# Windowed attention and a mixture-of-depths layer on one core: value matmul in two 64-column tiles, sinks in two 32-row tiles, double PSUM banks, loads in another order

## The chip, the core and the metric

The kernel runs on one core of a Trainium2 chip. A core has five engines, each with its own in-order instruction stream: TensorE (PE, matrix products into PSUM, the accumulator memory of eight banks), VectorE (DVE), ScalarE (ACT), GpSimd (POOL) and SyncE (SP, which here only issues transfers). PEld is TensorE's load of the stationary operand (the weights of a matmul), shown apart from the matmul (PE) that streams the moving operand past it. Sixteen DMA engines move data between the device's memory and SBUF, the on-chip memory; transfers are issued on POOL's queue, which may change the type on the way, or on SP's. The metric is the device time of one execution in microseconds (us), lower is better.

## The reference

Attention in which each query sees 128 keys up to its own and the first four keys (the sinks), followed by a layer that lets only the 128 tokens with the highest score of each batch through a small network.

```
B, H, S, D = 4, 8, 768, 64;  n_sink, window = 4, 128
scores = (q @ k^T) / sqrt(D)
keep = (pos_k < n_sink) | ((0 <= pos_q - pos_k) & (pos_q - pos_k < window))
a = exp(where(keep, scores, -1e9) - max);  a = a / (sum(a) + 1e-9)
x = concat_heads(a @ v)                      # (4, 768, 512)
# layer: w1 is 512 x 1024, w2 is 1024 x 512, capacity 128
s = x @ w_gate;  top = the 128 tokens of a batch with the largest s
out = x;  out[top] = x[top] + sigmoid(s[top]) * (relu(x[top] @ w1) @ w2)
```

## The kernel before

**Staging.** q and k of a batch come through POOL's queue, cast from f32 to bf16 (`load_qk`, L77: four pieces of 192 KB each for batch 0, one of 768 KB each for the others); v and the sinks' v come as f32 through SP's (`load_v`, L87 and L89). `transposes` (L147) turns 128 x 64 blocks of q and k on TensorE, two heads into the two halves of a tile of PSUM (64 output partitions, hence 64 weight columns, each), and DVE and ACT copy the result to KT and QT; the first four keys go to `ksk`.

**Attention.** The work runs over 24 units (b, j): batch b, block j of 128 queries. `scores` (L170, L177, L180) computes for a block kc of keys the transposed scores of its own and the next query block, for four heads at a time (group g): keys are the output's partitions, so the exponentials `pt` are the weights of the value matmul without another transpose. ACT takes the exponential from one bank (512 columns) at a time; POOL zeroes what the window excludes (L184, L188). `sink_scores` does the sinks of a whole batch at once. `pv` (L214) multiplies: weights `pt` (128 keys x 128 queries, f32), moving operand v of one head and a column of ones (65 columns, f32), output 128 queries x 65 columns, whose last column is the softmax's sum. A unit has 16 such matmuls (8 where j is 0), since the window spans two key blocks. The sinks' part of a unit is one matmul for each group (L206), 128 weight rows of which most are zero, 260 columns. `finish_block` divides by the sum (L223, L225), computes the score s (L228) and a bf16 copy (L231).

**Layer.** `moe_gen` is a generator: the layer of batch b is fed in steps, two in each unit, between the matmuls of batch b + 1; that of the last batch runs at the end alone. Its steps: broadcast s over partitions (dg on DVE L243, bc on TensorE L244, sbc on ACT L246); rank every token by counting greater scores, six times one DVE pass over 768 columns (L254) and a comparison that makes a one-hot block E (L257); transpose E (etp, L263); gather the chosen tokens (xeT, L271); w1 and Relu (hps, L290, L292); w2 (ye, L296); scatter back (ops, L303) and add x (o_sb, L305); store.

**Order.** In each unit the code writes the scores of the next unit ahead of `pv` of this one, then `finish_block`, then one pair of heads of the next batch's transposes (units 1 to 4). The build's scheduler places instructions on each engine, by data dependences and free buffers, and may move them from where the code writes them; from there on every engine runs its stream in order. Buffers: `sc_ps` two tiles of one bank (scores), `x_ps` two tiles of two banks (value), `mo_ps` two tiles of one bank (transposes and everything of the layer).

Of the kernel before, what the change touches and what calls it, by code (L numbers as in the profile page):

```python
# [15 lines left out]
H = 8  # L16
S = 768
# [11 lines left out]
def kernel(  # L29
# [27 lines left out]
    x_ps = ctx.enter_context(tc.tile_pool(name="x_ps", bufs=2, space=bass.MemoryType.PSUM))  # L57
    mo_ps = ctx.enter_context(tc.tile_pool(name="mo_ps", bufs=2, space=bass.MemoryType.PSUM))
# [3 lines left out]
    vsk = [vp.tile([128, H, VS], FP32, name=f"vsk{i}", tag=f"vsk{i}") for i in range(2)]  # L62
# [19 lines left out]
    def load_v(st):  # L82
        b = st.b
        st.v = vbuf[b % 2]
        st.vsk = vsk[b % 2]
        for h in range(H):
            nc.sync.dma_start(out=st.vsk[4 * h:4 * h + 4, h, 0:D], in_=v[b, h, 0:NSINK, :])  # L87
        for c in range(NB):
            nc.sync.dma_start(out=st.v[:, c, :, 0:D],  # L89
                              in_=v[b, :, c * 128:(c + 1) * 128, :].rearrange("h p d -> p h d"))  # L90

    st0 = load_qk(0, 4)

# [12 lines left out]
    for i in range(2):  # L106
        nc.gpsimd.affine_select(
            out=vsk[i][0:32, :, D:D + 1].rearrange("p h o -> p (h o)"),
            in_=ones_f[0:32, 0:H], compare_op=ALU.is_ge, fill=0.0, base=0,
            pattern=[[-4, H]], channel_multiplier=1)  # L110
        nc.gpsimd.affine_select(
            out=vsk[i][0:32, :, D:D + 1].rearrange("p h o -> p (h o)"),
            in_=vsk[i][0:32, :, D:D + 1].rearrange("p h o -> p (h o)"),
            compare_op=ALU.is_ge, fill=0.0, base=3,
            pattern=[[4, H]], channel_multiplier=-1)
    load_v(st0)
# [21 lines left out]
    def transposes(st, hp):  # L138
# [4 lines left out]
        for src, dst, eng in ((st.kb, st.KT, "v"), (st.qb, st.QT, "s")):  # L143
            trp = mo_ps.tile([128, NB, 128], BF16, name="trp", tag="mo")
            for c in range(NB):
                for e in range(2):
                    nc.tensor.transpose(out=trp[64 * e:64 * e + 64, c, :], in_=src[:, 2 * hp + e, c, :],  # L147
                                        identity=ident_b[:])
            o = dst[:, hp, :].rearrange("d (p c) -> d p c", c=NB)
            i = trp[:, :, :].rearrange("d c p -> d p c")  # L150
            if eng == "v":
# [3 lines left out]
        for e in range(2):  # L155
            nc.vector.tensor_copy(
                out=st.ksk[64 * e:64 * e + 64, hp, 8 * hp + 4 * e:8 * hp + 4 * e + 4],
# [3 lines left out]
    def scores(st, kc, g):  # L161
# [4 lines left out]
        banks = [sc_ps.tile([128, 2, 256], FP32, name="sc", tag="sc") for _ in range(2)]  # L166
        for hh in range(2):
            for e in range(2):
                hp = 2 * g + hh
                nc.tensor.matmul(  # L170
                    out=banks[e][:, hh, 0:nq],
# [3 lines left out]
        for e in range(2):  # L175
            if kc == 0:
                nc.tensor.matmul(out=banks[e][:, :, :], lhsT=ident_b[:, :], rhs=mask0[:, :, :],  # L177
                                 start=False, stop=True, skip_group_check=True)
            po = pt[:, 4 * g:4 * g + 4, :].rearrange("p (a e) n -> p e a n", e=2)
            nc.scalar.activation(out=po[:, e, :, 0:nq], in_=banks[e][:, :, 0:nq],  # L180
                                 func=ACT.Exp, scale=0.125)
# [10 lines left out]
    def sink_scores(st):  # L192
        st.psk = sp.tile([128, 512], FP32, name="psk", tag="psk")
        sk = mo_ps.tile([128, 512], FP32, name="sk", tag="mo")
        for hp in range(HP):
            nc.tensor.matmul(out=sk[:, :], lhsT=st.ksk[:, hp, :], rhs=st.QT[:, hp, 256:S],  # L196
                             start=(hp == 0), stop=(hp == HP - 1))
        nc.scalar.activation(out=st.psk[:, :], in_=sk[:, :], func=ACT.Exp, scale=0.125)

    def pv(st, j, g):  # L200
        if g == 0:
            st.xg = x_ps.tile([128, 2, 512], FP32, name="xg", tag="xg")
        xg = st.xg
        first = True
        if j >= 2:
            nc.tensor.matmul(out=xg[:, g, 0:4 * VS], lhsT=st.psk[:, (j - 2) * 128:(j - 1) * 128],  # L206
                             rhs=st.vsk[:, 4 * g:4 * g + 4, :].rearrange("p h e -> p (h e)"),
                             start=True, stop=False, skip_group_check=True)
            first = False
        for hh in range(4):  # L210
            h = 4 * g + hh
            terms = [(j, 0)] if j == 0 else [(j - 1, 128), (j, 0)]
            for kc, off in terms:
                nc.tensor.matmul(out=xg[:, g, hh * VS:(hh + 1) * VS],  # L214
                                 lhsT=st.pt[kc][:, h, off:off + 128],
                                 rhs=st.v[:, kc, h, :], start=first, stop=(hh == 3 and kc == j),
                                 skip_group_check=True)
                first = False

    def finish_block(st, j):  # L220
# [166 lines left out]
```

## Time and profile before

| | |
|---|---|
| median of 3 runs | 237.33 us (237.24 to 238.42) |
| profiled execution | 238.03 us, span 236.3 us |
| busy, share of the span | PE 83%, PEld 65%, DVE 50%, ACT 38%, POOL 25% |
| mean granted TensorE clock | 0.888 of full speed |
| chain that ended last | PE 74% (of the span: value matmul L214 36%, sinks 8%, scores 7%), waits for `kb` 12%, DVE 5% |
| transfers | 21.56 MB, 91 GB/s mean |

The span runs from the first to the last instruction. Busy time is the time in which an engine had an instruction under way, whatever else was waiting; matmuls are pipelined, and their ends are modelled, so a fully busy PE isn't an array at its peak. The chain is the sequence of work and waits that ended last, followed back from the end. The granted clock is 1.00 at 2.4 GHz and 0.50 at 1.2.

### The profile page before, as it was taken

What the parts mean: (1) busy time and instruction counts of PE and PEld (TensorE: products, weight loads), DVE (VectorE), ACT (ScalarE), POOL (GpSimd) and SP (SyncE); (2) the same over time, 40 slices, a digit from 0 to 9 for tenths busy, and PEclk for the clock granted to TensorE, in tenths of its full rate; (3) what the DMA queues carried; (4) which work ended last, traced back from release to release, by engine and by line L of the source; (5) the groups of instructions that cost most, each with busy time, mean ns of one, the idle gap of its engine ahead of it and who ended that gap; (6) DMA issues with size and microseconds to landing.
All of it is one profiled execution on the core that took longest, in us unless ns stands there. A gap on an engine that the chain in (4) does not pass through costs nothing.

```text
span 236.3 us, 4345 instructions
## 1 busy us (share of the span) xinstructions
PE 196.0 (83%) x1752; PEld 154.7 (65%) x1752; DVE 118.5 (50%) x292; ACT 90.4 (38%) x169; POOL 59.1 (25%) x101
## 2 busy tenths in 40 slices
PE   0369701999999999999999999999999999944850
PEld 0344401887887888887878788777888977922810
DVE  3542100330444199853746896287399607488032
ACT  2124700232354474454365545544465533120210
POOL 8901410032225046223103442210054223000000
PEclk9999955555699999999999999999999999985595
DMA  7999999995122991202434000033000004200024
GB/s 108 182 200 199 194 191 219 206 188 97 46 47 48 181 177 44 46 1 68 186 109 89 0 3 3 0 137 133 0 3 0 3 0 163 106 0 0 4 106 162
DMA packets 38821, 21.56 MB, mean 91 GB/s; under 512 B 25872, under 2 KB 35088, under 8 KB 38800
## 3 DMA queue, kind: packets, MB, share of 16 engines
q0 software_dynamic: 9984, 8.39, 23.1%
q1 hardware_dynamic: 28816, 12.88, 21.8%
q8 instruction: 14, 0.23, 0.4%
q14 instruction: 7, 0.06, 0.1%
HBM read 23.36 MB, written 6.29 MB: 125 GB/s over the span
## 4 chain that ended last, share of the span: by engine, by line
PE 74%; DMA 13%; DVE 5%; POOL 4%; issue 1%; ACT 1%; POOLq 0%; DVEq 0%
PE xg L214 36%; DMA kb<-in_k_dram 12%; PE xg L206 8%; PE sc L170 7%; PE trp L147 5%; PE hps L290 4%; PE ye L296 3%; PE bc L244 3%; PE xeT L271 3%; DVE cjunk L254 2%; PE ops L303 2%; PE sc L177 1%; POOL qb L77 1%; POOL kb L77 1%; PE sk L196 1%; DVE o_sb L305 1%
## 5 line engine op out<-in xcount | busy, mean ns | idle before, releaser
L214 PEld LDWEIGHTS xg<-vbuf,pt 128*128 128x128 f32 x704 | 92.9, 205 | 8.6 <-issue 5.4
L214 PE MATMUL xg<-vbuf,pt 128*128 128x65 f32 x704 | 96.7, 289 | 0.0
L180 ACT ACTIVATE pt<-sc 128x512 f32<-128x512 f32 (+1 forms) x96 | 50.3, 562 | 53.6 <-PE sc L170 47.2
L184 POOL TENSOR_SCALAR_AFFINE_SELECT pt<-pt 128x512 f32<-128x512 f32 x40 | 25.6, 641 | 131.8 <-ACT pt L180 131.8
L223 DVE RECIPROCAL rz<-xg 128x8 f32<-128x8 f32 x24 | 4.9, 205 | 65.4 <-PE xg L214 65.3
L147 PE MATMUL trp<-ident_b,kb 128*64 128x128 bf16 x192 | 10.4, 257 | 22.5 <-DMA kb<-in_k_dram 14.3
L154 ACT COPY QT<-trp 128x768 bf16<-128x768 bf16 x16 | 12.8, 802 | 32.8 <-PE trp L147 32.8
L254 DVE TENSOR_SCALAR_CACHE_REDUCE cjunk<-sbc,scol 128x768 f32<-128x768 f32 x24 | 24.1, 1004 | 1.8 <-ACT sbc L246 1.8
L170 PE MATMUL sc<-QT,KT 64*128 64x256 bf16 (+1 forms) x192 | 24.3, 281 | 0.7 <-ACT pt L180 0.7
L147 PEld LDWEIGHTS <-kb 128*64 128x64 bf16 x192 | 7.4, 130 | 25.2 <-DMA kb<-in_k_dram 22.4
L228 DVE CUSTOM_DVE_ANT_0 junk<-x,wgb 128x512 f32<-128x512 f32 x24 | 16.5, 687 | 14.7 <-DMA wgb<-in_moe_w_gate_dram 14.4
L206 PE MATMUL xg<-vsk,psk 128*128 128x260 f32 x64 | 22.5, 435 | 0.0
L305 DVE TENSOR_TENSOR o_sb<-ops,x 128x512 f32<-128x512 f32 x24 | 15.7, 688 | 10.9 <-PE ops L303 9.5
L188 POOL TENSOR_SCALAR_AFFINE_SELECT pt<-pt 128x512 f32<-128x512 f32 x32 | 20.3, 634 | 0.0
L152 DVE COPY KT<-trp 128x768 bf16<-128x768 bf16 x16 | 15.3, 954 | 8.8 <-PE trp L147 8.8
L231 ACT CAST xb<-x 128x512 bf16<-128x512 f32 x24 | 14.8, 619 | 9.8 <-DVE x L225 9.8
L225 DVE TENSOR_TENSOR x<-xg,rz 128x512 f32<-128x512 f32 x24 | 16.5, 686 | 0.4
L206 PEld LDWEIGHTS xg<-vsk,psk 128*128 128x128 f32 x64 | 10.7, 196 | 5.0 <-issue 2.5
L170 PEld LDWEIGHTS <-KT 64*128 64x128 bf16 x192 | 7.1, 95 | 10.4 <-issue 6.6
L147 PE MATMUL trp<-ident_b,qb 128*64 128x128 bf16 x192 | 10.8, 256 | 1.1 <-DVE KT L152 1.1
L263 PE MATMUL etp<-ident_b,E 128*128 128x128 bf16 x24 | 5.7, 237 | 6.2 <-DVE E L257 6.2
L303 PE MATMUL ops<-gye,ET 128*128 128x512 bf16 x24 | 8.3, 380 | 3.0 <-DVE o_sb L305 2.3
(57 smaller groups left out, 164.4 us busy)
## 6 DMA issues: line engine op xcount, KB each, us to landing
vbuf<-in_v_dram SPq DMA_DIRECT2D x24, 256.0 KB
out_dram<-o_sb SPq DMA_DIRECT2D x24, 256.0 KB
qb<-in_q_dram POOLq DMA_DIRECT2D x3, 768.0 KB, 24.4
kb<-in_k_dram POOLq DMA_DIRECT2D x3, 768.0 KB, 9.1
w_sb<-in_moe_w_dram POOLq DMA_DIRECT2D x2, 1024.0 KB, 16.9
qb<-in_q_dram POOLq DMA_DIRECT2D x4, 192.0 KB, 7.7
kb<-in_k_dram POOLq DMA_DIRECT2D x4, 192.0 KB, 8.4
vsk<-in_v_dram SPq DMA_DIRECT2D x32, 1.0 KB
```

Of the source, the lines that this page charges most:

```text
L147: nc.tensor.transpose(out=trp[64 * e:64 * e + 64, c, :], in_=src[:, 2 * hp + e, c, :], identity=ident_b[:])
L152: nc.vector.tensor_copy(out=o, in_=i)
L170: nc.tensor.matmul(out=banks[e][:, hh, 0:nq], lhsT=st.KT[64 * e:64 * e + 64, hp, kc * 128:(kc + 1) * 128], rhs=st.QT[64 * e:64 * e + 64, h ...
L180: nc.scalar.activation(out=po[:, e, :, 0:nq], in_=banks[e][:, :, 0:nq], func=ACT.Exp, scale=0.125)
L184: nc.gpsimd.affine_select(out=pt[:, hs, 0:128], in_=pt[:, hs, 0:128], compare_op=ALU.is_ge, fill=0.0, base=0, pattern=[[0, 4], [1, 128]], ...
L188: nc.gpsimd.affine_select(out=pt[:, hs, 128:256], in_=pt[:, hs, 128:256], compare_op=ALU.is_ge, fill=0.0, base=-1, pattern=[[0, 4], [-1, 1 ...
L206: nc.tensor.matmul(out=xg[:, g, 0:4 * VS], lhsT=st.psk[:, (j - 2) * 128:(j - 1) * 128], rhs=st.vsk[:, 4 * g:4 * g + 4, :].rearrange("p h e ...
L214: nc.tensor.matmul(out=xg[:, g, hh * VS:(hh + 1) * VS], lhsT=st.pt[kc][:, h, off:off + 128], rhs=st.v[:, kc, h, :], start=first, stop=(hh ...
L225: nc.vector.tensor_tensor(out=xn, in0=xv[:, :, :, 0:D], in1=rz[:, :, :, :].to_broadcast((128, 2, 4, D)), op=ALU.mult)
L228: nc.vector.tensor_tensor_reduce(out=junk[:, :], in0=st.x[:, j, :], in1=wgb[:, :], scale=1.0, scalar=0.0, op0=ALU.mult, op1=ALU.add, accum ...
L254: nc.vector.tensor_scalar(out=cjunk[:, :], in0=sbc[:, :], scalar1=scol[:, c:c + 1], scalar2=0.0, op0=ALU.is_gt, op1=ALU.add, accum_out=ran ...
L305: nc.vector.tensor_tensor(out=o_sb[:, :], in0=ops[:, :], in1=st.x[:, c, :], op=ALU.add)
```

## The change

- **Value matmul** (`pv`): each product is split by its queries into two matmuls of 64 weight columns, m = 0 into the PSUM partitions 0 to 63, m = 1 into 64 to 127, both with the same 65 moving columns. Groups have their own tile of one bank (`x_ps`, three of them); the reciprocal and the division are done for each group, right behind its matmuls.
- **Sinks**: the sinks' weights and values of the groups lie in rows 0 to 31 and 32 to 63, and `pv_sinks` issues both groups' matmuls in a row, ahead of `pv`, each on 32 rows.
- **Banks**: `sc_ps` holds two tiles of two banks, used by the scores of four heads (one Exp over 1024 columns instead of two over 512), the transposes (k and q in one tile), the sinks' scores, bc (one tile and one copy for six blocks), hps (one tile, one Relu over 1024 columns) and ops (two blocks and one addition over 1024 columns at a time). `mo_ps` is one bank, for etp, xeT, se and ye.
- **Order**: the scores of both groups of the next unit are written ahead of this unit's value matmuls; `sink_scores` of a batch comes behind its unit 0; w1 and w2 are loaded in the program's second unit; v of batch 0 is loaded through POOL's queue, right behind q and k.

```diff
-    x_ps = ctx.enter_context(tc.tile_pool(name="x_ps", bufs=2, space=bass.MemoryType.PSUM))
-    mo_ps = ctx.enter_context(tc.tile_pool(name="mo_ps", bufs=2, space=bass.MemoryType.PSUM))
+    x_ps = ctx.enter_context(tc.tile_pool(name="x_ps", bufs=3, space=bass.MemoryType.PSUM))
+    mo_ps = ctx.enter_context(tc.tile_pool(name="mo_ps", bufs=1, space=bass.MemoryType.PSUM))
...
+    load_v(st0, nc.gpsimd)
...
-            trp = mo_ps.tile([128, NB, 128], BF16, name="trp", tag="mo")
+        trp = sc_ps.tile([128, 2, 8, 128], BF16, name="trp", tag="sc")
...
-        banks = [sc_ps.tile([128, 2, 256], FP32, name="sc", tag="sc") for _ in range(2)]
+        sc = sc_ps.tile([128, 2, 2, 256], FP32, name="sc", tag="sc")
...
-            nc.scalar.activation(out=po[:, e, :, 0:nq], in_=banks[e][:, :, 0:nq],
-                                 func=ACT.Exp, scale=0.125)
+        nc.scalar.activation(out=po[:, :, :, 0:nq], in_=sc[:, :, :, 0:nq], func=ACT.Exp, scale=0.125)
...
+    def pv_sinks(st, j):
+        st.xg = [x_ps.tile([128, 4, VS], FP32, name="xg", tag="xg") for _ in range(2)]
+        if j < 2:
+            return
+        for g in range(2):
+            nc.tensor.matmul(out=st.xg[g][:, :, :], lhsT=st.psk[32 * g:32 * g + 32, (j - 2) * 128:(j - 1) * 128],
+                             rhs=st.vsk[32 * g:32 * g + 32, :, :],
+                             start=True, stop=False, skip_group_check=True)
...
     def pv(st, j, g):
...
             for kc, off in terms:
-                nc.tensor.matmul(out=xg[:, g, hh * VS:(hh + 1) * VS],
-                                 lhsT=st.pt[kc][:, h, off:off + 128],
-                                 rhs=st.v[:, kc, h, :], start=first, stop=(hh == 3 and kc == j),
-                                 skip_group_check=True)
-                first = False
+                for m in range(2):
+                    nc.tensor.matmul(out=xg[64 * m:64 * m + 64, hh, :],
+                                     lhsT=st.pt[kc][:, h, off + 64 * m:off + 64 * m + 64],
+                                     rhs=st.v[:, kc, h, :],
+                                     start=(j < 2 and hh == 0 and kc == terms[0][0]),
+                                     stop=(hh == 3 and kc == j), skip_group_check=True)
+        rz = sp.tile([128, 4, 1], FP32, name="rz", tag="rz")
+        nc.vector.reciprocal(out=rz[:, :, :], in_=xg[:, :, D:D + 1])
+        nc.vector.tensor_tensor(
+            out=st.x[:, j, 256 * g:256 * g + 256].rearrange("p (h d) -> p h d", h=4),
+            in0=xg[:, :, 0:D], in1=rz[:, :, :].to_broadcast((128, 4, D)), op=ALU.mult)
...
+        bc = sc_ps.tile([128, 2, 512], FP32, name="bc", tag="sc")
...
+        hps = sc_ps.tile([128, 8, 128], FP32, name="hps", tag="sc")
...
+            ops = sc_ps.tile([128, 2, DM], FP32, name="ops", tag="sc")
...
+            nc.vector.tensor_tensor(out=o_sb[:, :, :], in0=ops[:, :, :], in1=st.x[:, 2 * half:2 * half + 2, :], op=ALU.add)
...
-    nc.gpsimd.dma_start(out=w1_sb[:], in_=moe_w1.rearrange("(dc p) f -> p dc f", p=128))
-    nc.gpsimd.dma_start(out=w2_sb[:], in_=moe_w2.rearrange("(fc p) d -> p fc d", p=128))
...
+        if u == 1:
+            nc.gpsimd.dma_start(out=w1_sb[:], in_=moe_w1.rearrange("(dc p) f -> p dc f", p=128))
+            nc.gpsimd.dma_start(out=w2_sb[:], in_=moe_w2.rearrange("(fc p) d -> p fc d", p=128))
...
-        for g in range(2):
-            if nxt:
-                scores(states[nxt[0]], nxt[1], g)
+            for g in range(2):
+                scores(states[nxt[0]], nxt[1], g)
+        pv_sinks(st, j)
+        for g in range(2):
             pv(st, j, g)
```

What the scheduler made of it is seen at two places. The first is TensorE's stream in unit 1 of batch 1, where the layer's transposes of the one-hot blocks (etp) stand between the value matmuls (xg) and the scores (sc). Before:

```order
L214 MATMUL xg<-vbuf_95,pt 128x65 x3
L263 LDWEIGHTS E
L263 MATMUL etp<-ident_b,E 128x128
L170 LDWEIGHTS KT
L170 MATMUL sc<-QT,KT 128x256
L170 LDWEIGHTS KT
L170 MATMUL sc<-QT,KT 128x256
L214 MATMUL xg<-vbuf_95,pt 128x65 x5
L263 LDWEIGHTS E
L263 MATMUL etp<-ident_b,E 128x128
L271 LDWEIGHTS xb
L271 MATMUL xeT<-E,xb 128x128
```

In the change, at the same place (trp is the transpose of the next batch's keys):

```order
L214 MATMUL xg<-vbuf_95,pt 64x65 x5
L259 LDWEIGHTS E
L259 MATMUL etp<-ident_b,E 128x128
L214 MATMUL xg<-vbuf_95,pt 64x65 x7
L259 LDWEIGHTS E
L259 MATMUL etp<-ident_b,E 128x128
L214 MATMUL xg<-vbuf_95,pt 64x65 x9
L145 LDWEIGHTS kb
L145 MATMUL trp<-ident_b,kb 64x128
```

Each value matmul stands there twice, once for each half of the queries; the transposes of E still stand in TensorE's stream between them, so a block E that is late on DVE holds back what is behind it.

The second place is POOL's stream at the program's start, before against change: the loads of v of batch 0 (vbuf), and of w1 and w2 (w_sb) and q and k of batch 1 (qb, kb).

```order
 L77 DMA kb<-in_k_dram 128x2x384
+L90 DMA vbuf_94<-in_v_dram 128x8x64 x6
 masks.py:197 MEMSET ident_f 128x128
...
-L129 IOTA iota_i 128x128
-L322 DMA w_sb<-in_moe_w_dram 128x4x1024
-L323 DMA w_sb<-in_moe_w_dram 128x8x512
+L127 IOTA iota_i 128x128
 L77 DMA qb<-in_q_dram 128x8x384
 L77 DMA kb<-in_k_dram 128x8x384
+L329 DMA w_sb<-in_moe_w_dram 128x4x1024
+L330 DMA w_sb<-in_moe_w_dram 128x8x512
```

The six loads of v now stand ahead of the identity matrix (ident_f) that the first transposes need, and w1 and w2 stand behind the keys of batch 1. On SP's queue the gate's weights and v of batch 1 take the place of v of batch 0.

## Rows read from the trace of the kernel before

**Rows 1.** Windows by stage: stretch and length, busy us (records) by engine, clock, DMA

```profile
0.00:29.60 29.60, 16.19 (x144) 9.86 (x144) 9.83 (x26) 11.07 (x17) 14.96 (x31) 1.00 1.12 177
29.60:40.45 10.85, 0.00 (x0) 0.00 (x0) 0.00 (x0) 0.00 (x0) 0.83 (x2) 0.50 1.27 205
40.45:63.76 23.31, 23.30 (x135) 19.19 (x135) 6.67 (x18) 6.92 (x12) 4.49 (x7) 0.50 0.84 144
63.76:75.14 11.38, 11.38 (x132) 9.70 (x132) 3.65 (x10) 3.99 (x10) 4.07 (x7) 1.00 0.12 27
75.14:118.99 43.85, 43.82 (x439) 35.22 (x440) 28.93 (x70) 21.96 (x42) 12.54 (x20) 1.00 0.49 103
118.99:162.65 43.66, 43.66 (x439) 35.31 (x440) 29.23 (x71) 22.14 (x42) 11.13 (x18) 1.00 0.19 56
162.65:206.20 43.55, 43.55 (x375) 36.30 (x376) 25.65 (x64) 20.35 (x40) 11.13 (x18) 1.00 0.12 43
206.20:236.33 30.13, 14.06 (x95) 9.08 (x93) 14.55 (x36) 4.02 (x8) 0.00 (x0) 0.69 0.14 53
```

**Rows 2.** Timeline, first 48 us: start, length, instruction, count, idle time before and releaser

```profile
4.23 20.96 SPq L89 DMA_DIRECT2D vbuf<-in_v_dram  x5
...
8.23 0.85 PE L147 MATMUL trp<-ident_b,kb 128*64 128x128 bf16 x12 [8.23 <-DVE ident_b L98]
...
9.66 0.96 POOL L323 DMA_DIRECT2D w_sb<-in_moe_w_dram  x1
...
11.40 0.96 POOL L77 DMA_DIRECT2D kb<-in_k_dram  x1
...
40.45 0.85 PE L147 MATMUL trp<-ident_b,kb 128*64 128x128 bf16 x12 [11.95 <-DMA kb<-in_k_dram]
```

**Rows 3.** DMA queues of the page: packets, MB, share of 16 engines' span

```profile
q0 software_dynamic: 9984, 8.39, 23.1%
q1 hardware_dynamic: 28816, 12.88, 21.8%
```

**Rows 4.** Chain that ended last: start, length, engine, tile, line, records

```profile
76.51 0.44 PE xg L206 x2
77.17 1.73 PE xg L214 x16
...
100.05 0.79 PE trp L147 x24
...
102.32 1.79 PE hps L290 x32
```

**Rows 5.** One line's records from 100 to 165 us: ns min/median/max

```profile
L214 PEld LDWEIGHTS xg<-vbuf,pt x248: 186/192/192, 100.8 to 165.0; 128*128 128x128 f32 x124
...
L147 PEld LDWEIGHTS <-kb x96: 106/110/110, 100.0 to 161.7; 128*64 128x64 bf16 x96
...
L290 PEld LDWEIGHTS <-w_sb x64: 97/98/153, 102.0 to 147.5; 128*128 128x128 bf16 x64
```

**Rows 6.** Timeline around the rank computation of batch 1, in batch 2's stage

```profile
130.26 0.48 ACT L246 COPY sbc<-bc 128x384 f32<-128x384 f32 x1 [0.99 <-PE bc L244]
...
141.40 0.78 PE L271 MATMUL xeT<-E,xb 128*128 128x128 bf16 x11
```

**Rows 7.** Window inside the rank computation, columns as in rows 1

```profile
130.00:140.00 10.00, 10.00 (x87) 8.23 (x87) 9.35 (x24) 5.97 (x11) 4.04 (x8) 1.00 0.01 2
```

**Rows 8.** Groups by form: count, busy us, mean ns, idle before, releasers

```profile
L214 PE MATMUL xg<-vbuf,pt 128*128 128x65 f32 x704 | 96.7, 289 | 0.0
...
L180 ACT ACTIVATE pt<-sc 128x512 f32<-128x512 f32 x80 | 45.0, 599 | 45.1 <-PE sc L170 38.7 <-PE sc L177 6.3
...
L225 DVE TENSOR_TENSOR x<-xg,rz 128x512 f32<-128x512 f32 x24 | 16.5, 686 | 0.4
L305 DVE TENSOR_TENSOR o_sb<-ops,x 128x512 f32<-128x512 f32 x24 | 15.7, 688 | 10.9 <-PE ops L303 9.5 <-DMA out_dram<-o_sb 1.3
...
L180 ACT ACTIVATE pt<-sc 128x256 f32<-128x256 f32 x16 | 5.3, 382 | 8.5 <-PE sc L170 8.5
...
L223 DVE RECIPROCAL rz<-xg 128x8 f32<-128x8 f32 x24 | 4.9, 205 | 65.4 <-PE xg L214 65.3
```

More of the change, by code (lines that the diff above doesn't have):

```diff
@@ L197, in sink_scores @@
                              start=(hp == 0), stop=(hp == HP - 1))
-        nc.scalar.activation(out=st.psk[:, :], in_=sk[:, :], func=ACT.Exp, scale=0.125)
-    def pv(st, j, g):
[L201 to L208, printed above, removed]
-            first = False
+        nc.scalar.activation(out=st.psk[:, :], in_=sk[0:64, 0, :], func=ACT.Exp, scale=0.125)
@@ L284, in moe_gen @@
         hT = mp.tile([128, 8, 128], BF16, name="hT", tag="hT")
-        for fq in range(2):
-            hps = mo_ps.tile([128, 4, 128], FP32, name="hps", tag="mo")
-            for f4 in range(4):
-                fc = 4 * fq + f4
-                for dc in range(4):
-                    nc.tensor.matmul(out=hps[:, f4, :], lhsT=w1_sb[:, dc, fc * 128:(fc + 1) * 128],
-                                     rhs=xeT_sb[:, dc, :], start=(dc == 0), stop=(dc == 3))
-            nc.scalar.activation(out=hT[:, 4 * fq:4 * fq + 4, :], in_=hps[:, :, :], func=ACT.Relu)
-            yield
+        hps = sc_ps.tile([128, 8, 128], FP32, name="hps", tag="sc")
+        for fc in range(8):
+            for dc in range(4):
+                nc.tensor.matmul(out=hps[:, fc, :], lhsT=w1_sb[:, dc, fc * 128:(fc + 1) * 128],
+                                 rhs=xeT_sb[:, dc, :], start=(dc == 0), stop=(dc == 3))
+        nc.scalar.activation(out=hT[:, :, :], in_=hps[:, :, :], func=ACT.Relu)
+        yield
         ye = mo_ps.tile([128, DM], FP32, name="ye", tag="mo")
@@ L300, in moe_gen @@
         yield
-        for c in range(NB):
-            ops = mo_ps.tile([128, DM], FP32, name="ops", tag="mo")
-            nc.tensor.matmul(out=ops[:, :], lhsT=ET[:, c, :], rhs=gye[:, :], start=True, stop=True)
-            o_sb = op.tile([128, DM], FP32, name="o_sb", tag="o_sb")
-            nc.vector.tensor_tensor(out=o_sb[:, :], in0=ops[:, :], in1=st.x[:, c, :], op=ALU.add)
-            nc.sync.dma_start(out=out[b, c * 128:(c + 1) * 128, :], in_=o_sb[:, :])
-            if c == 2:
+        for half in range(3):
+            ops = sc_ps.tile([128, 2, DM], FP32, name="ops", tag="sc")
+            for e in range(2):
+                nc.tensor.matmul(out=ops[:, e, :], lhsT=ET[:, 2 * half + e, :], rhs=gye[:, :], start=True, stop=True)
+            o_sb = op.tile([128, 2, DM], FP32, name="o_sb", tag="o_sb")
+            nc.vector.tensor_tensor(out=o_sb[:, :, :], in0=ops[:, :, :], in1=st.x[:, 2 * half:2 * half + 2, :], op=ALU.add)
+            for e in range(2):
+                c = 2 * half + e
+                nc.sync.dma_start(out=out[b, c * 128:(c + 1) * 128, :], in_=o_sb[:, e, :])
+            if half == 0:
                 yield
```

96 lines of the change are left out of this document (42 added, 54 removed).

## The prediction

> **What bounds the kernel now.** I cut the span into stages first [rows 1]. From 75.1 to 206.2 us TensorE (PE) is busy for the whole of every stage, while VectorE (DVE) is busy for 29 of 43.7 us and ScalarE for 22: three batches at 43.85, 43.66 and 43.55 us, bound by PE. Ahead of that stand a stage of 10.85 us in which no compute engine does anything while the DMA engines are full, and one of 23.31 us in which PE is busy throughout at a granted clock of 0.50 (1.2 GHz). Behind it come 30.13 us in which PE works 14.06.
>
> The start's timeline says what the empty stage waits for [rows 2]: PE stands until 40.45 us for the keys of batch 1 (`kb`). Their load was issued at 11.40, but behind the two weight loads on the same queue, the second issued at 9.66, and beside SyncE's loads of `v`.
>
> The chain of waits then shows what PE's time buys [rows 4]. 16 records of the value matmul take 1.73 us, 0.108 each; every matmul is two records (704 [rows 8] for 352). The sink matmul streams 260 columns in 0.22, or 0.85 ns a column, so the 65 value columns need only 0.055. The rest is the weight load: loading 128 columns of f32 is reported at 192 ns, of bf16 at 98 [rows 5], so the f32 load spends at least 94 ns on its columns. The load sets the pace; the stream hides under it.
>
> **What the change is worth, part by part.**
>
> *Value matmul.* 352 matmuls become 704, each of 64 weight columns and the same 65 moving ones; each is again two records. No row shows a 64-column f32 load. From columns alone I estimate half of 0.108, 0.054, the same as its stream. So two records of one tile would take 0.108 in a row. What counts is whether the other tile's two run beside them. The nearest rows are the transposes, which already alternate between two 64-column tiles: 24 in 0.79 us, 0.033 each, while the 128-column matmul that streams as many columns takes 0.056 (32 in 1.79) [rows 4]. So streams of two column tiles do run side by side; that their loads do too isn't shown, since a bf16 load is short. The bounds for a pair of 64-column matmuls are then 0.108 (tiles side by side) and 0.216 (one after the other), against 0.216 for the one matmul today. I take 0.108, by the transposes: 0.108 saved for each of today's matmuls.
>
> The Trainium skill (TensorE: Matmul & The Clock Gate, Part 3, "The mechanism") says that a weight load overlaps a running matmul only when their row groups differ. Two column tiles share their rows, so by that rule load and stream would add up, 0.054 + 0.054 for each of four records, 0.43 a pair: twice today's price. The rows speak against it: load (at least 94 ns) and stream (55) of today's value records use the same rows and would sum to 0.149, and the record takes 0.108.
>
> *Sinks.* Two 128-row matmuls of 0.44 become two on 32 rows, into different banks. If the second's first record runs beside the first's last, three slots of 0.22 remain of four: 0.22 saved a unit. Bounds 0 and 0.44.
>
> *Start.* The second order piece shows the keys of batch 1 ahead of the weights, but behind the six `v` loads that moved to this queue; SyncE now carries `v` of batch 1. Price by queue [rows 3]: the POOL queue's 8.39 MB took 23.1% of 236.3 us, 6.5 us per MB of all 16 engines; SyncE's 12.88 MB took 21.8%, 4.0 us per MB. Before, until `kb` landed: 1.57 + 2.10 + 1.57 MB at 6.5 and 1.83 MB at 4.0, together 41.4 us of engine time in the 38.4 us since about 2 us, a share of 1.08. Now: q and k of batch 0 (10.2), `v` of batch 0 at SyncE's price (6.3), q and k of batch 1 (10.2), the gate and `v` of batch 1 on SyncE (7.3): 34.0, at 1.08 31.5 us, landing at 33.5. Upper bound, `v` at the POOL queue's price (10.2): 37.1. Lower, half of SyncE's `v` still to come: 30.4. So **-6.9 us**. The six issues (0.9 each, as the load of `kb`) push the identity and the first transpose (8.23) to about 13.5, and the first scores wait for the last q and k piece anyway, so this hides in the stall.
>
> *From `kb` to 75.14.* 23.31 us at half clock and 11.38 at full are 23.0 us of full-clock work. The stages hold the value matmuls of units 1 to 4. Unit 1's 16 now stand ahead of the stall (16 x 0.216 = 3.5); the 48 of units 2 to 4 save 5.2, three units' sinks 0.7. Left 13.7. The clock fell while PE stood still and came back at 63.76, after 23.3 us in which PE was busy throughout [rows 1]. What the slow clock costs now is bounded by 0 (it returns with the work) and 13.7 (it stays to the stage's end). No row decides; before it returned, PE ran value records whose stream fills half of each, and side by side they would follow each other as the transposes do. I choose 3.3, near the low end, which is 6.6 us at half clock. 17.0 us instead of 34.7: **-17.7 us**.
>
> *Batches 1 and 2.* Each has 88 value matmuls; 32 of them, units 1 and 2, lie beside the rank computation, which DVE does in six steps, each ending in a transpose on PE. There the sum of PE's savings doesn't count. In the stage of batch 2 the last broadcast ended at 130.26 + 0.48, and PE could begin its long xeT run at 141.40 [rows 6]: 10.7 us, with DVE 9.35 of 10 us busy [rows 7]. DVE's work there doesn't shrink: evacuating x in two halves costs two reciprocals and two half multiplies, about 2 x (0.205 + 0.42) for 0.205 + 0.686 [rows 8], 0.36 more a unit. I put the stretch at 9.9, so 0.8 is saved instead of 3.9. The other 56 matmuls save 6.05, three units' sinks 0.66. Against that 0.8 of new waits: scores, transposes, `bc`, `hps` and `ops` now share two double banks; `ops` in pairs needs one DVE add of 1.24 (0.688 for 512 columns) before a later tile gets the bank, and the one Relu of 1024 columns (599 + 2 x 217 ns, by the two Exp forms) holds `ye` back. -6.7 each, **-13.4 us**. The merged Exp saves ScalarE some 2 us a batch, and nobody waits for ScalarE long.
>
> *Batch 3's stage* holds 104 matmuls; 72 outside the stretch save 7.8, four units' sinks 0.9, the stretch 0.8, less 0.4 of waits: **-9.1 us**. *Tail:* Relu and the broadcast in one piece each cost 0.4 and 0.3, the smaller last multiply gives 0.3 back: **+0.4 us**; the rank computation on DVE stays.
>
> Sum: -6.9 - 17.7 - 13.4 - 9.1 + 0.4 = -46.7. The profiled execution took 238.03 with a span of 236.33, so 1.7 lies around the span; 189.6 + 1.7 = 191.3. The profiled one stands 0.7 above the median: **191 us**.
>
> **Rivals.**
>
> *Half overlap.* The four records of a pair come as tile A, A, B, B. The transposes alternate with every record, so they don't show this order. If A's second record holds B's first back, a pair costs about 0.162: 0.054 on 232 matmuls (48 + 2 x 56 + 72) is 12.5 more, **204 us**.
>
> *The tiles take turns* (0.216): the value matmul gains nothing. 232 x 0.108 = 25 more, and the stream stays as thin as now, so I let the slow clock cost 8 us more, as near the high end: **224 us**. For it: no row shows two f32 loads at once.
>
> *The clock falls between batches.* PE would work about 7 of the 9.9 us of each rank stretch and wait for DVE in the rest. In the tail the clock fell with PE at 14.06 of 30.13. One fall of 10 to 15 us in each batch would cost about 8: **215 us**.
>
> *Slower.* If a 64-column record costs what a 128-column one does, 0.108, and the tiles take turns, a pair is 0.432. Beside the 224 case that is 0.054 on 4 x 328 records behind the stall, 71 us: **295 us**. It decides from (237.3 - 224) / 1312 = 0.010 us above 0.054, so from 0.064 a record. Against it: the load's time follows its columns' bytes in [rows 5] (192 for f32, 98 for bf16). For it: the bf16 load of 64 columns is reported longer (110) than that of 128. This is also where the skill's rule on row groups would end: its 0.43 a pair is this rival's price, and the trace of before speaks against its premise.
>
> **Chances and range.** Tiles side by side, 191 us: 0.60; its own range, from the bounds of the start (-3, +4), of the clock (-3, +10) and 1.5 us a batch of waits either way, is 182 to 207. Half overlap 0.15, turns 0.12, clock falls 0.06, slower 0.03, and 0.04 for under 182 (sinks at 0.44, DVE's stretch hidden). From 181 to 222 lie nearly all of the first, the second and the fourth, and the edge of the third: about 0.8. A difference of 0.5% is what a measurement can tell here. All cases but the slower one (and a clock that falls everywhere, 0.01) are faster: 0.95; same 0.01; slower 0.04.
>
> **What will show it.** The value records: 64-column records at about 0.027 each in the chain or the spacing of a run of them (0.054 means turns, 0.04 half). `kb` of batch 1: PE's first transpose behind the stall at 33.5. The clock: full within 7 us of that. The rank stretch: still about 10 us, with PE now idle in parts and DVE named as the releaser of `etp` and xeT. Batches at about 37 us. If batches fall under 34, DVE was no limit; if they stay above 41, the tiles take turns.

## The result, and the profile after

The changed kernel took 201.49 us (median of 4 runs, 201.09 to 201.83) beside 237.69 us for the kernel before on the same chip: a ratio of 0.847, 95% interval 0.8445 to 0.8503. 191 us was forecast, with a range of 181 to 222. The profiled execution has a span of 199.40 us. On the other chips used below the kernel before took 236.5 to 238.3 us in some executions and 242.0 to 249.5 in others; the ratios below are to the first kind, so a time between the two does not show a loss.

The stages, cut at the same events as in [rows 1] (the keys of batch 1, the first mask matmul of each later batch, the last value matmul). Columns: stretch and length, busy us (records) of PE, its weight loads, DVE, ScalarE, POOL, then clock, DMA share and GB/s:

```profile
0.00:33.72 33.72, 15.96 (x225) 10.42 (x226) 12.25 (x35) 11.19 (x13) 23.33 (x44) 1.00 1.13 187
33.72:47.90 14.18, 13.44 (x317) 10.50 (x318) 10.25 (x30) 8.95 (x12) 7.38 (x13) 1.00 1.20 198
47.90:88.66 40.76, 39.05 (x619) 26.97 (x618) 29.84 (x81) 21.80 (x29) 12.78 (x20) 1.00 0.90 170
88.66:128.94 40.28, 38.56 (x616) 26.75 (x616) 29.15 (x80) 21.10 (x28) 11.04 (x18) 1.00 0.19 58
128.94:169.21 40.27, 38.52 (x595) 27.06 (x593) 26.28 (x74) 18.93 (x25) 11.20 (x18) 0.96 0.11 41
169.21:199.40 30.19, 12.33 (x94) 7.96 (x94) 13.83 (x33) 3.88 (x6) 0.00 (x0) 0.76 0.14 53
```

Set against [rows 1], the stretch up to the keys lost 6.7 us (40.45 to 33.72), the one from the keys to batch 1's stage 20.5 (34.69 to 14.18), and the three batches 3.1, 3.4 and 3.3 each. More than half of the gain lies in the second row: the clock column reads 1.00 there, where it read 0.50 for 23.31 us. The records' own times bear that out. In the kernel before, in the stretch at 0.50:

```profile
42.34 3.25 PE L214 MATMUL xg<-vbuf,pt 128*128 128x65 f32 x14
```

That is 0.232 us a record, where [rows 4] has 0.108. The 1.00 of the first row, here and in [rows 1], is no such reading: the trace holds no clock record ahead of 27.9 us (22.8 in the kernel before), and the transposes there run at about half the pace (24 in 1.49 us below, 24 in 0.79 in [rows 4]).

The timeline of the start, as in [rows 2]:

```profile
7.11 5.50 POOL L90 DMA_DIRECT2D vbuf<-in_v_dram  x6
...
13.60 1.49 PE L145 MATMUL trp<-ident_b,kb 128*64 128x128 bf16 x24 [13.60 <-DVE ident_b L104]
...
16.61 0.90 POOL L77 DMA_DIRECT2D kb<-in_k_dram  x1
17.48 0.78 POOL L329 DMA_DIRECT2D w_sb<-in_moe_w_dram  x1
...
33.72 0.47 PE L145 MATMUL trp<-ident_b,kb 128*64 128x128 bf16 x10 [0.65 <-DMA kb<-in_k_dram]
```

The six issues of `v` hold the first transpose back to 13.60 us, the keys of batch 1 are issued 5 us later than before and land 6.7 us earlier, and PE, itself late, stands 0.65 us for them instead of 11.95.

The chain of waits in the first units behind the keys, and in batch 2's stage (start, length, engine, tile, line, records):

```profile
36.15 2.04 PE xg L214 x64
...
89.20 0.46 PE trp L145 x12
89.66 0.63 PE xg L203 x2
90.29 0.38 PE xg L214 x6
...
98.55 0.81 ACT sbc L243
99.38 1.03 DVE cjunk L250 x2
100.44 0.29 DVE E L253
100.72 0.93 DVE cjunk L250 x2
...
109.75 1.45 PE xeT L267 x24
```

64 records, which are 16 of the former value matmuls, take 2.04 us: 0.032 a record and 0.1275 a former matmul, where [rows 4] had 0.216. From start to start within the run, two records come every 58 ns (0.117 a former matmul). One record's 65 columns need about 55 ns by the forecast's working, so two records stream at once. Two sink records take 0.63 instead of 0.44. From the broadcast's end at 99.36 to the gather (`xeT`) the chain is DVE's counts (`cjunk`) and comparisons (`E`). One window over that stretch and the groups by form say the same:

```profile
99.36:109.75 10.39, 9.06 (x154) 6.19 (x150) 10.32 (x28) 5.08 (x6) 4.84 (x8) 1.00 0.01 2
```

```profile
L214 PE MATMUL xg<-vbuf,pt 128*64 128x65 f32 x1408 | 60.8, 231 | 0.0
L214 PEld LDWEIGHTS xg<-vbuf,pt 128*64 128x64 f32 x1408 | 51.2, 142 | 14.4 <-issue 12.3
```

DVE is busy 10.32 of 10.39 us there. The load of 64 f32 columns is reported at 142 ns (192 for 128 in [rows 5]).

### The profile page after: what moved, and what is told of

Read it like the earlier page. It is cut to its first block, busy times and chain, and to the rows that moved or that the text cites. A ratio compares the mean times of both kernels' runs of the same rounds, so it can differ in the third digit from the quotient of the medians.

```text
span 199.4 us, 5721 instructions
## 1 busy us (share of the span) xinstructions
PE 157.9 (79%) x2456; PEld 109.7 (55%) x2456; DVE 121.6 (61%) x328; ACT 85.9 (43%) x113; POOL 65.7 (33%) x111
## 4 chain that ended last, share of the span: by engine, by line
PE 52%; DVE 20%; DMA 9%; POOL 7%; ACT 6%; issue 3%; DVEq 1%; ACTq 0%; POOLq 0%
PE xg L214 18%; DVE cjunk L250 11%; DMA kb<-in_k_dram 9%; PE xg L203 6%; PE ye L290 4%; PE bc L241 4%; PE hps L284 4%; PE trp L145 4%; PE xeT L267 4%; DVE E L253 3%; PE sc L169 3%; PE ops L298 3%; POOL vbuf L90 2%; ACT pt L179 2%; POOL qb L77 2%
## 5 line engine op out<-in xcount | busy, mean ns | idle before, releaser
L214 PE MATMUL xg<-vbuf,pt 128*64 128x65 f32 x1408 | 60.8, 231 | 0.0
L214 PEld LDWEIGHTS xg<-vbuf,pt 128*64 128x64 f32 x1408 | 51.2, 142 | 14.4 <-issue 12.3
L179 ACT ACTIVATE pt<-sc 128x1024 f32<-128x1024 f32 (+1 forms) x48 | 44.8, 953 | 22.2 <-PE sc L169 15.9
L220 DVE RECIPROCAL rz<-xg 128x4 f32<-128x4 f32 x48 | 8.6, 179 | 35.7 <-PE xg L214 35.5
L145 PE MATMUL trp<-ident_b,kb 128*64 128x128 bf16 x192 | 10.2, 244 | 14.7 <-DVE ident_b L104 13.6
L221 DVE TENSOR_TENSOR x<-xg,rz 128x256 f32<-128x256 f32 x48 | 20.2, 422 | 1.2
L169 PE MATMUL sc<-QT,KT 64*128 64x256 bf16 (+1 forms) x192 | 19.2, 273 | 0.7 <-ACT pt L179 0.2
L203 PE MATMUL xg<-vsk,psk 32*128 32x260 f32 x64 | 19.6, 429 | 0.0
L300 DVE TENSOR_TENSOR o_sb<-ops,x 128x1024 f32<-128x1024 f32 x12 | 14.5, 1220 | 6.4 <-PE ops L298 6.4
L152 ACT COPY QT<-trp 128x768 bf16<-128x768 bf16 x16 | 12.7, 798 | 3.0 <-PE trp L145 2.5
L145 PE MATMUL trp<-ident_b,qb 128*64 128x128 bf16 x192 | 10.2, 244 | 3.6 <-DVE KT L150 3.5
L145 PEld LDWEIGHTS <-qb 128*64 128x64 bf16 x192 | 8.0, 124 | 7.3 <-issue 7.0
L203 PEld LDWEIGHTS xg<-vsk,psk 32*128 32x128 f32 x64 | 8.2, 183 | 5.4 <-issue 3.6
```

The source lines that it names most:

```text
L145: nc.tensor.transpose(out=trp[64 * e:64 * e + 64, t, c, :], in_=src[:, 2 * hp + e, c, :], identity=ident_b[:])
L169: nc.tensor.matmul(out=sc[:, e, hh, 0:nq], lhsT=st.KT[64 * e:64 * e + 64, hp, kc * 128:(kc + 1) * 128], rhs=st.QT[64 * e:64 * e + 64, hp, ...
L179: nc.scalar.activation(out=po[:, :, :, 0:nq], in_=sc[:, :, :, 0:nq], func=ACT.Exp, scale=0.125)
L203: nc.tensor.matmul(out=st.xg[g][:, :, :], lhsT=st.psk[32 * g:32 * g + 32, (j - 2) * 128:(j - 1) * 128], rhs=st.vsk[32 * g:32 * g + 32, :, ...
L214: nc.tensor.matmul(out=xg[64 * m:64 * m + 64, hh, :], lhsT=st.pt[kc][:, h, off + 64 * m:off + 64 * m + 64], rhs=st.v[:, kc, h, :], start=( ...
L221: nc.vector.tensor_tensor(out=st.x[:, j, 256 * g:256 * g + 256].rearrange("p (h d) -> p h d", h=4), in0=xg[:, :, 0:D], in1=rz[:, :, :].to_ ...
```

## The experiments

Theories ahead of them. (A) The two column tiles run side by side, and this is the gain. (B) DVE's rank computation sets the time of units 1 and 2 of each batch. (C) The sinks on 32 rows cost time. (D) The order of the loads gives the start. Rivals: PE's changes from one tile shape to another eat the gain; DVE doesn't matter; `v` on POOL's queue is itself a cost. Stage lengths compare well between chips: batch 2's stage was 40.28, 40.29 and 40.29 us in the change and in e6 and e9 (both below), whose code is the same from there on. No run takes out the double banks and the merged steps by themselves.

**The tiles: taken out of the change, and put alone into the kernel before.**

```diff
 e1_no_tiles (the change, without them)
-for m in range(2):
-    nc.tensor.matmul(out=xg[64 * m:64 * m + 64, hh, :],
-                     lhsT=st.pt[kc][:, h, off + 64 * m:off + 64 * m + 64], ...
+nc.tensor.matmul(out=xg[:, hh, :], lhsT=st.pt[kc][:, h, off:off + 128], ...
 e4_tiles_alone (the kernel before, with them)
-nc.tensor.matmul(out=xg[:, g, hh * VS:(hh + 1) * VS], lhsT=st.pt[kc][:, h, off:off + 128], ...
+for m in range(2):
+    nc.tensor.matmul(out=xg[64 * m:64 * m + 64, g, hh * VS:(hh + 1) * VS],
+                     lhsT=st.pt[kc][:, h, off + 64 * m:off + 64 * m + 64], ...
```

> The changed kernel, but each value matmul again as one tile of 128 columns; sinks, banks, load order and all else as in the change. Tiles side by side are the gain: a value matmul costs 0.216 us again instead of the 0.116 that its two halves take in the changed kernel's trace, 0.100 on 232 matmuls behind the stall, 23 us: 224.5 us, and batches at 40.4 + 56 x 0.100 = 46 us. If changes of tile shape on TensorE give back a large part of what the narrow tiles win: some 215 us, batches at 43. If in addition the clock comes back late again as in the kernel before: up to 8 us more, and a row of granted clock 0.50 behind the stall.

> The kernel before, but each value matmul as two tiles of 64 columns side by side; nothing else changed. If the tiles are worth the full 0.100 a matmul: 248 matmuls lie behind the stall, 16 of them and more at half clock, so 25 to 29 us: 210 us. If the rank computation on DVE and the changes of tile shape take half of that: 223 us. The stall before the keys of batch 1 must stay, at about 40 us, by both.

Without the tiles, 244.5 us: 1.033 times the kernel before (1.0275 to 1.0382), no gain at all, and not clearly a loss. The tiles alone, 213.39 us (0.900, 0.8956 to 0.9042). So the tiles are worth 43 us in the changed kernel and 24 in the kernel before. I had expected 23 and 25 to 29. Windows over batch 2's stage of the kernel without tiles (columns as above) show where much of the other 20 us comes from:

```profile
106.47:123.70 17.23, 16.92 (x154) 13.57 (x152) 12.81 (x39) 10.14 (x13) 4.93 (x9) 1.00 0.22 48
123.70:137.40 13.70, 13.70 (x79) 11.12 (x77) 6.53 (x20) 2.66 (x4) 2.35 (x4) 0.50 0.01 1
137.40:157.93 20.53, 20.53 (x212) 15.20 (x211) 9.94 (x22) 8.35 (x13) 3.66 (x6) 1.00 0.21 78
```

Within the rank stretch (117.4 to 134.2 us here) the clock falls to 0.50 (1.2 GHz) and stays there for 13.7 us, with PE busy for 16.92 of the 17.23 us before the fall. It falls so in every batch (10.2, 13.7 and 13.7 us in the clock's records); at half pace these 37.6 us cost up to 18.8. In the change, at the same place, it fell once in three batches, for 3.4 us. The kernel before has the wide matmul too, and in its profiled execution the clock did not fall in the batches ([rows 1]); so in these traces the falls come with the wide matmul and the rest of the change together. The same in the start, by the page's rows of granted clock in 40 slices, the kernel with the tiles alone:

```profile
PEclk9999995579999999999999999999999999975596
```

PE's stand before the keys is that of the kernel before (11.65 us, the clock falls in it), but the clock is back at 44.9 us, 4.4 us after the keys; in [rows 1] it took 23.3. Of this kernel's 24 us, 15 come from the stage behind the keys (40.54 to 60.21 us, 19.7 against 34.7), 3.0, 3.2 and 3.3 from the batches:

```profile
60.21:101.01 40.80, 38.32 (x617) 26.88 (x615) 28.48 (x71) 21.94 (x43) 12.94 (x20) 1.00 0.55 113
101.01:141.49 40.48, 38.02 (x616) 26.79 (x615) 28.42 (x71) 21.94 (x43) 11.47 (x18) 1.00 0.19 56
```

(A) holds, and the tiles give twice: by their own time, and by the clock. The same rows say what the rest of the change is worth beside the tiles. Batches 1 and 2 take 40.76 and 40.28 us in the change, 40.80 and 40.48 here, so the double banks, the merged steps and the sinks on 32 rows together give 0.2 us a batch at most; the 12 us between the two kernels lie ahead of batch 1's stage, which begins at 47.90 instead of 60.21.

**The load order alone.** In the kernel before, `v` of batch 0 goes to POOL's queue and the weights behind the keys:

```diff
 e3_loads_alone
+load_v(st0, nc.gpsimd)
 ...
-load_v(st0)
 ...
-nc.gpsimd.dma_start(out=w1_sb[:], ...)
-nc.gpsimd.dma_start(out=w2_sb[:], ...)
+        if u == 1:  # both, here
```

> The kernel before with only the change's load order: v of batch 0 on POOL's queue behind q and k, the MoE weights behind the keys of batch 1. The keys of batch 1 should land at 33 to 34 us as in the changed kernel. If the gain of the order is that landing alone: 6.9 us, 230.5. If the shorter stand of TensorE also brings its clock back sooner, which in the kernel before stood at 0.50 until 63.76 us: up to 11 us more, 219 to 226. If the order is worth nothing without the narrow tiles: 237.

240.7 us, and nothing to conclude from the total: the four runs lie between 235.82 and 242.49. Of the profiled one (240.77) only the start is read here. PE's first transpose behind the keys stands at 32.73, 7.7 us earlier than before, and then:

```profile
32.73:72.90 40.17, 40.17 (x221) 31.62 (x222) 11.03 (x27) 13.21 (x24) 10.90 (x18) 0.50 0.74 124
```

40.2 us of work at the lower level, until past the time at which the kernel before had its clock back (63.76): in this execution the earlier keys are lost again. The shortest run (235.82, mean clock 0.894 against 0.867 in this one) is only 1.5 us below the median before. What the order alone is worth to a per cent stays open; a gain of 6.9 us is in none of the four runs. (D) fits the 12 us above, which lie in the start; without the tiles no gain from the order is shown.

**The count of the rank, shortened**, and **DVE's work handed to other engines**. The first leaves out five sixths of each count, so its chosen rows are not the reference's:

```diff
 e5_short_count
-nc.vector.tensor_scalar(out=cjunk[:, :], in0=sbc[:, :], ...
+nc.vector.tensor_scalar(out=cjunk[:, 0:128], in0=sbc[:, 0:128], ...
 e7_dve_relief
-nc.vector.tensor_scalar_mul(out=dg[:, :], in0=ident_f[:, :], scalar1=scol[:, j:j + 1])
+nc.scalar.activation(out=dg[:, :], in_=ident_f[:, :], func=ACT.Copy, scale=scol[:, j:j + 1])
-nc.vector.tensor_scalar(out=E[:, c, :], ...
+nc.gpsimd.tensor_scalar(out=E[:, c, :], ...
```

> The changed kernel, but the count of larger scores runs over 128 instead of 768 columns, which leaves out most of the rank computation, so the chosen rows are not the reference's. It takes about 0.7 us from each of six counts on DVE in each batch. If DVE paces the units with the rank computation: 2 to 4 us less in each of three batch stages and 4 in the tail, 187 to 191 us, the stretch from the broadcast to the gather at 6.5 to 8 us. If TensorE sets the time there all the same: the tail alone gains, 197.5 us, and the stretch stays near 10 us.

> The changed kernel, but the six products for the broadcast (dg) on ScalarE and the six comparisons for E on POOL, 6 x 0.397 and 6 x 0.334 us less for DVE in each batch, nothing left out. If DVE paces the units with the rank computation, as the shortened count suggests: 2 to 2.5 us less in each of three batches and 1.5 in the tail, 192 to 194 us. If the handing over between engines, or POOL's masks behind the comparisons, eats it: 200 to 203.

The short count took 191.4 us (0.806, 0.8012 to 0.8098), 10 less than the change. Its windows over batch 2's stage, and over the rank stretch within it:

```profile
89.10:126.75 37.65, 36.64 (x616) 25.81 (x615) 26.38 (x80) 21.14 (x29) 11.10 (x18) 1.00 0.21 64
99.86:105.75 5.89, 5.30 (x80) 3.41 (x76) 5.59 (x24) 3.25 (x5) 2.39 (x4) 1.00 0.02 4
```

The stretch falls from 10.39 to 5.89 us and the whole stage by 2.6 (40.28 to 37.65); the tail falls by 4.0. (B) holds, with a bound: of the 4.5 us by which the stretch shortens, the stage gains 2.6, and PE is then busy for 36.64 of 37.65 us. Handing work over instead made it slower, 207.7 us (0.874, 0.8687 to 0.8787). Its group of comparisons on POOL shows one reason:

```profile
L253 POOL TENSOR_SCALAR E<-iota_f,rank 128x128 bf16<-128x128 f32 x24 | 14.9, 622 | 20.0 <-DVE cjunk L250 20.0
```

622 ns for one that took DVE 334, between POOL's masks: the stretch grew to 12.3 us in batch 2. The other is the clock, which fell to 0.50 in the rank stretch of each batch, for 3.4, 3.4 and 10.2 us, where the change had 3.4 us in the last alone. How the loss divides between the two isn't shown.

**The sinks on 128 rows again**, values in tiles as in the change:

```diff
 e2_sinks128
-nc.tensor.matmul(out=st.xg[g][:, :, :], lhsT=st.psk[32 * g:32 * g + 32, ...], rhs=st.vsk[32 * g:32 * g + 32, :, :],
+nc.tensor.matmul(out=st.xg[g][:, :, :], lhsT=st.psk[:, ...], rhs=st.vsk[:, 4 * g:4 * g + 4, :],
 ...  # and the shapes and layouts of vsk, psk and ksk to match
```

> The changed kernel, but the sink matmuls on 128 zero-padded rows again, as in the kernel before; value tiles and all else as in the change. If the 32-row tiles cost time where the scheduler sets the two of a unit apart (a lone one 0.63 us against 0.44): about 1 us a batch back, 198 us, batches at 39.5. If they save as the prediction put it (0.22 a unit, 16 units): 205 us. If neither, because DVE sets the time there: 201.5.

201.17 us (198.77 to 204.63): the totals don't tell it from the change. The stages do:

```profile
49.35:89.39 40.04, 38.30 (x619) 27.46 (x617) 29.41 (x81) 21.54 (x29) 12.81 (x20) 1.00 0.87 166
89.39:129.09 39.70, 37.95 (x616) 27.10 (x615) 28.77 (x80) 21.05 (x29) 11.04 (x18) 1.00 0.20 62
```

0.72 and 0.58 us less than in the change. (C) holds in sign, at about two thirds of the 1 us expected. The chain of waits shows what the 32 rows cost. With 128 rows, in batch 2's stage:

```profile
115.43 0.64 PE xg L205 x2
...
122.33 0.54 PE ops L300 x2
122.87 0.44 PE xg L205 x2
123.31 0.43 PE ops L300 x2
```

and in the change, at the same place:

```profile
121.63 0.54 PE ops L298 x2
122.17 0.63 PE xg L203 x2
122.80 0.54 PE ops L298 x2
```

On 128 rows the sinks take 0.44 behind a matmul that fills the array (`ops`, `ye`, the mask) and 0.64 behind one that doesn't (transposes, values in tiles, scores); [rows 4] had shown one of the cheap kind, and five of the eight in that stage of the kernel before were of the dear one. On 32 rows they take 0.63 behind everything, and `ops` behind them 0.54 instead of 0.43: a change of tile on the array costs 0.1 to 0.2 us by these rows. In this run's start PE stood 2.61 us for the keys and the clock fell for 3.4 us; the stage behind them was 1.8 us longer (15.95 us to the same mark), which hides the gain in the total.

**Where `v` of batch 0 is loaded.** Back on SyncE's queue, without and with the gate's weights ahead of it:

```diff
 e6_v_on_sync
-load_v(st0, nc.gpsimd)
+load_v(st0)
 e9_gate_first (also)
+wgb = cp.tile([128, DM], FP32, name="wgb", tag="wgb")
+nc.sync.dma_start(out=wgb[:], in_=moe_w_gate.partition_broadcast(128))
 load_v(st0)
```

> The changed kernel, but v of batch 0 on SyncE's queue again, so POOL makes the identity at 8 instead of 13 us. If the keys of batch 1 set the start: they still land at 33 to 34 us, TensorE stands some 5 us longer before them and the time stays at 201.5, or 203 to 205 if its clock falls in that stand. If the late identity costs time that the stall does not hide: 197 to 199.

> The changed kernel, but v of batch 0 on SyncE's queue as before, and the gate's weights (wgb) ahead of it there. In the run with v on SyncE the keys of batch 1 were there by 27.9 us and DVE stood 18.1 us for wgb. If wgb behind v was all that cost there: no wait for wgb, the first mask of batch 1's stage at 42 instead of 47.84 us, 195 to 197 us. If v on SyncE costs by its bytes beside the keys: keys at 33 or later, 201 to 205, and 206 or more if TensorE's clock falls in the stand.

213.28 us (0.896, 0.8908 to 0.9019) and 206.69 us (0.868, 0.8629 to 0.872): both slower than the change, and neither for the reason that I had given. In the first the keys are there at 27.9 us, but two rows, of DVE's waits and of PE's timeline, show this:

```profile
DVE junk L227 <- DMA wgb<-in_moe_w_gate_dram: 18.1, 1, 18.1
```

```profile
44.77 1.20 PE L203 MATMUL xg<-vsk,psk 32*128 32x260 f32 x2 [15.31 <-issue]
```

`junk` needs the gate's weights, which lie behind `v` on SyncE's queue; DVE stands until 43.0, can't free the accumulators `xg`, and PE stands for them. (PE's own row names no releaser; its sinks start at 44.77, 0.11 us behind the first division of `xg` on DVE.) With the weights ahead that wait is gone and the keys are there at 27.15. Batch 1's stage begins at 44.83 instead of 47.84, and then PE's waits give it back, more than whole:

```profile
PE xg L214 <- DMA vbuf<-in_v_dram: 10.9, 3, 8.0
...
44.83:95.61 50.78, 40.80 (x613) 28.75 (x616) 29.65 (x81) 21.71 (x29) 12.57 (x20) 0.90 0.78 154
```

Three waits for `v`, the longest, 8.0 us, for that of batch 1, and around its end 10.2 us of slow clock (53.7 to 64.0): 10.0 us more in that stage. In the change PE's waits name no `v` in its first 60 us. The queues share the DMA engines (a share of 1.11 up to the keys, 1.22 from there to batch 1's stage, 1.26 from there to 59 us, the end of these waits), so what is moved ahead is paid by what it is moved ahead of.

**Two ways to spread the counts, and combinations.**

```diff
 e10_rank_spread / e13_pairs (e13 also with the sinks on 128 rows)
-            if c == 2:
+            if c < 5:          # e13: if c in (1, 3):
                 yield
 e8_together:  e2's, e6's and e7's edits, v of batch 1 on POOL's queue behind its keys
 e12_together: e2's, e9's and e10's edits
```

> The changed kernel, but the six counts of the rank computation are written one to each half unit instead of three, the layer's other steps behind them, nothing left out. DVE then has one count of 1.09 us and one comparison of 0.33 in a half unit of some 3.3 us. If DVE's load in those two units is what holds TensorE: 1 to 2.5 us less in each of three batches, 194 to 198 us. If a late E holds TensorE's stream wherever it stands: 201 or more.

> The changed kernel with the sinks on 128 rows and the rank counts written two to a half unit instead of three (one step more for the layer, not four). With one to a half unit, the three stretches of the batches together were 5.6 us shorter than in the changed kernel, and 6.9 us came back behind the last value matmul, because the layer of batch 2 ended late. If half of the gain is had with two and little comes back: 2 to 3 us, and 2 from the sinks, 196 to 198. If what is gained in the batches comes back at the end again: 200 to 202. The start's loads are those of the changed kernel, so the keys of batch 1 land at 33 to 34 us by both.

> The changed kernel with the sinks on 128 rows, dg on ScalarE, E on POOL, v of batch 0 on SyncE and v of batch 1 on POOL's queue behind the keys of batch 1. If each does what its theory says: 8 us from DVE's relief, 2 from the sinks and 4 to 5 from keys that land at 28 to 29 us, 186 to 188 us. If the keys are bound by all bytes in flight and not by their order: 190 to 192. If the relief of DVE is eaten: 195 or more.

> The changed kernel with the gate's weights ahead of v of batch 0 on SyncE, the sinks on 128 rows and the rank counts one to a half unit. If all three theories hold: 5.8 us from the start, 2 from the sinks, 3 to 7 from the spread counts, 187 to 191 us. If only the start and the sinks: 193 to 194. If TensorE's clock falls in the start's stand: 200.

One count to a half unit: 204.12 us (0.860, 0.8556 to 0.8636). Its windows over the last batch's stage and the tail:

```profile
126.82:165.04 38.22, 36.28 (x595) 25.48 (x598) 26.31 (x73) 18.88 (x26) 10.94 (x18) 1.00 0.12 43
165.04:202.10 37.06, 16.88 (x97) 10.96 (x98) 16.39 (x36) 3.89 (x6) 0.00 (x0) 0.64 0.23 86
```

The three batches took 37.67, 39.92 and 38.22 us, 5.5 less in all, and the tail 6.9 more: the layer of batch 2 ends late, its output adds stand on DVE ahead of batch 3's broadcast, which ends 7.4 us behind the last value matmul instead of 3.7, and the clock is at 0.64 on the mean instead of 0.76. Two to a half unit gained nothing: 203.47 us (0.860, 0.8542 to 0.8654), the batches at 41.13, 40.62 and 38.73, the tail at 33.98. There the broadcast ends 3.7 us behind the last value matmul, as in the change, so the tail's 3.8 us more are not a late layer's: the clock falls to 0.50 for 23.9 us instead of 10.2, and `hps` and `ye` take 3.45 and 3.61 us instead of 1.82 and 1.92. The combinations took 222.23 us (0.938, DVE again without the gate's weights, for 22.4 us) and 206.8 us (0.867, batch 1's stage at 49.21 with the wait for `v`). None of these beats the changed kernel.

## Why the prediction was right, and where its sizes were off

*The value matmul.* Mechanism right: two column tiles run side by side, and e1 and e4 show that they carry the gain. A pair was put at 0.108 and takes 0.1275 in a run of 64 (0.117 inside it). The rule on row groups of the Trainium skill (TensorE: Matmul & The Clock Gate, Part 3, "The mechanism") would have made it 0.43, as the forecast worked it out; the trace speaks against its use for these tiles, which share their rows. Half overlap (0.162) and turns (0.216) fall with it.

*The start, -6.9.* 33.5 us forecast for the keys, 33.72 measured, and the late identity did hide in the stall. But why it was worth that was only half seen. Beside the keys, DVE stood 14.4 us for the gate's weights in the kernel before, until 41.5; moving `v` off SyncE's queue took away both waits, and e6 shows what is left when only the first goes. That the sum of bytes met the landing to 0.2 us is luck in part: with the same bytes, `v` of batch 0 on SyncE, it gives 33.5 again, and the keys were there at 27.9 (e6) and 27.15 (e9).

*From the keys to batch 1's stage, -17.7.* It was -20.5. The work was put at 13.7 and the slow clock at 3.3; with a stand of 0.65 us the clock did not fall, and the stage took 14.18. So in the change the low price had another cause than the one given, a fall that did not come. That the clock comes back sooner with the tiles, the reason given, is borne out by e4 (4.4 us behind the stand), e9 (5.0), e6 (5.4) and e8 (10.4), against 23.3 us with the wide matmul; that it is the density of the stream which does it isn't shown.

*Batches 1 and 2, -6.7 each: the step that failed, by its size.* Measured -3.1 and -3.4. In batch 2, 3.3 us are missing. The sinks: -0.66 was taken, e2 shows that they cost 0.58, which makes 1.2. The value matmuls outside the rank stretch: 56 x (0.1275 - 0.108) is 1.1. The stretch: from the broadcast's end to the long `xeT` run 10.66 us before [rows 6], 10.39 after, 0.3 saved of 0.8, which makes 0.5. That is 2.8 of 3.3. The last 0.5 is argued, not shown: short runs of value records cost more a record than long ones (6 in 0.38, 0.063 each), as they would if every change of tile had the price that the sinks show. The sum left that price out. All of the stage's value records bear the size out, counted from each one's start to the next record's, waits included: 88 matmuls took 20.42 us before and 15.26 in the change, 0.059 saved each where the forecast had 0.108 for 56 of them; with the short count, where DVE holds them back less, 14.17, or 0.071 each. That DVE paces the stretch was right (e5).

*Batch 3, -9.1.* Measured -3.3: the same three, for 72 value matmuls (1.4) and four units' sinks, and a stretch that grew, to 11.8 us, with a slow clock of 3.4 us in it. *The tail, +0.4:* 30.19 for 30.13.

*The rivals.* "The clock falls between batches" did not happen in the change beyond those 3.4 us, but it is what happens in e1, one fall of 10 to 14 us in each batch, as that rival had priced it. Against e1 it is the tiles that held it off, which the forecast had not tied together; they don't always, since in e7 the clock fell for 10.2 us in the last batch with the tiles in place.

*The total.* The span shrank by 36.9 us where the sum had 46.7. The three batches gave 12.7 less than forecast, and 2.9 came back elsewhere, almost all in the stage behind the keys. The result stands nearer to half overlap (204) than to the forecast's own case (191), but its mechanism isn't that one: half overlap needed 0.04 a record, and a long run shows 0.032.

## What to carry over

Where a matmul's weight load sets its pace, try it as two column tiles, price it by its short runs as well as its long ones, and look at the clock besides: here the tiles also brought it back sooner after a stand, and in the changed kernel kept it from falling in the batches but for 3.4 us. Before you cost an earlier transfer, list every wait that ends near it on every engine (here the keys at 40.45 and the gate's weights at 41.5 us), and what it is moved ahead of. When an engine off PE paces a stretch, look at who works for the next stretch before you shift its work: spread, it came back in the tail, in part as a slower clock; handed over, on a slower engine.

## What was not expected of the hardware

- With the same value work, the granted clock came back 4.4 us after the keys with 64-column tiles (e4) and 23.3 us after them with 128-column ones (the kernel before); behind other stands with tiles it took from 3.2 (e2) to 10.4 us (e8). Within batches it fell for 10 to 14 us in all three with the wide ones and the rest of the change (e1), in none of the profiled kernel before, and once, for 10.2 us, with tiles (e7).
- The clock's records don't cover everything. Ahead of 27.9 us the change's trace has none, and the column reads 1.00 there. Four executions of the kernel before at 237.3 to 237.6 us are listed with a mean clock of 0.96, others of the same time with 0.89; no trace of the four is kept, so why they differ stays open.
- Two f32 records of a sink took 0.44 us behind a matmul on the whole array and 0.64 behind one on a part of it; on 32 rows 0.63 behind either.
- The same comparison of 128 x 128 elements took 622 ns on POOL and 334 on DVE; the product with a column 395 ns on ScalarE and 397 on DVE.
